# One block's attention among another block's MLP matmuls: another placement of the same work

## The chip, the cores and the metric

The kernel runs on one core of a Trainium2 chip. The metric is the device time of one execution in microseconds. Three executions of the kernel before gave 277.17, 277.19 and 277.25 us; the median is 277.19 us. Differences are read against that spread. The engines of the core work side by side, each through its own queue in order: TensorE (PE in the profile; its weight loads are PEld), VectorE (DVE), ScalarE (ACT), GpSimd (POOL) and SyncE (SP), whose queue only issues DMAs here. They meet through semaphores.

## The reference

Two layers in a row. First attention in blocks: for every batch element and head, an 8 x 8 matrix is normalized over rows and columns five times, and mixes the eight 96-row blocks of k and of v. Each block of q then attends to its own mixed block.

```python
for _ in range(5):
    P = np.exp(P - np.max(P, axis=-1, keepdims=True))
    P = P / (np.sum(P, axis=-1, keepdims=True) + 1e-09)
    P = P / (np.sum(P, axis=-2, keepdims=True) + 1e-09)
k_sorted = np.einsum('bhij,bhjcd->bhicd', P, k_b)
v_sorted = np.einsum('bhij,bhjcd->bhicd', P, v_b)
attn = softmax(scale * q_b @ k_sorted_b^T)          # within a block of 96
x = attn @ v_sorted_b                               # 4 x 768 x 512 after heads are joined
```

Then a residual MLP: a token mixing and a channel MLP.

```python
a1 = alpha1 * x + beta1
u = x + lam * np.einsum('ts,bsd->btd', w_tok, a1)
a2 = alpha2 * u + beta2
out = u + lam * (np.maximum(a2 @ w_ch1, 0.0) @ w_ch2)
```

There are 4 batch elements, 8 heads, 768 rows, head size 64, model width 512 and hidden width 2048.

## The kernel before

Every function of the kernel issues instructions through small wrappers on the engines that keep TensorE, VectorE, ScalarE and GpSimd in the order in which the program writes them (all those instructions carry line 65 in the profile, so they are told apart by tile names). DMAs that SyncE issues are not held to that order; a scheduler places them in SP's queue.

Batch element 0 has its attention done first, on its own (to about 40 us). From then on the program is a loop over batch elements b, which this text calls blocks, and over two halves `hf` of the 768 rows. A half has 16 **h units** (`h_unit`: four matmuls of 128x384 into one PSUM tile `h_ps`, then a relu on ScalarE into `hTa` or `hTb`) and 3 **ch units** (`ch_unit`: 16 matmuls of 128x512 into `ch_ps`, then the output: a multiply on VectorE into `ost`, an add on GpSimd, two DMAs out on SP).

All other work is hung between these units by a table. `put(b, hf, kind, n, ...)` (line 791) files a piece of work under a block, a half, a kind of unit ("h" or "c") and a number; `run` issues what is filed right after that unit. In the kernel before, a ch unit is cut into four parts of four matmuls, so that "c" has the numbers 0 to 11. The order within one place is the order of the `put` calls.

During block p the work of the attention of b = p + 1 is:

- `mix_matrix(b)`: a small product `repv_ps`, and six VectorE instructions that make the mixing matrices `bigM` and `bigP`. In the kernel before b = 1 is at h 10 of block 0, b = 2 and b = 3 at c 5 of half 1 of blocks 0 and 1.
- `mix_v(b, n)`, n = 0 to 2: two matmuls into `mix_ps`, then a VectorE cast of 128x1024 into `mixed`. `bounce_v` writes `mixed` to DRAM (`vscr`), `back_v` reads it back into `Vs` in another layout; both are SP's.
- `mix_k(b, n)`, n = 0 to 2: eight matmuls into `kmix_ps`, then four casts into `kT`. `q_turn_late(b, g)`, g = 0 to 3: six transposes into `qt_ps`, one copy into `qT`. These are in half 0's ch units.
- `score(b, g, hf)`, eight of them: eight matmuls into `sc_ps`, one exp on ScalarE into `et`. `pv(b, g, hf)`, eight: eight matmuls of `et` with `Vs` into `x_ps`, on VectorE a reciprocal (`rcb`), a multiply into `x`, and `first_affine`: two instructions that make `a` from `x`. In the kernel before these last two are kept back in the list `late` and issued by `flush` in the next pv, behind its multiply.
- `tails(x, lo, hi, ...)`: three VectorE copies that move rows of the last two blocks; for `a`, then for `x`.
- `moe_tok(b, kt)`: six matmuls of 128x512 into `tok_ps`, then `toktmp` and two additions into `u`. `moe_cross`: three DMA transposes of `u` into `uT`, on SP. `moe_affine`: four VectorE instructions from `uT` to `a2T`, which the next half's h units read.
- `load_kv(b + 1)` and `load_q(b + 1)`: POOL's loads for the next block.

Two PSUM pools bind these together. `psA` has two buffers of two banks each, used by `mix_ps`, `kmix_ps`, `sc_ps`, `x_ps` and `repv_ps`. `psB` has four buffers of one bank, used by `h_ps`, `ch_ps`, `tok_ps`, `qt_ps` and `back_ps`. A product can begin only when what was in its buffer has been read out.

In the scores and in pv the stationary operand has 128 columns wherever the tile has that many left, `w = min(128, ...)`, although a block has 96; the surplus rows of the output are not read. Both kernels do this.

Of the kernel before, what the change touches and what calls it, by code (L numbers as in the profile page):

```python
# [16 lines left out]
def kernel(  # L17
# [442 lines left out]
    def pv(b, g, hf):  # L460
# [17 lines left out]
            ps[0:BLK, :, :, 0:D].rearrange("p a k d -> p k a d"),  # L478
            rc[0:BLK].rearrange("p a k -> p k a").unsqueeze(3).to_broadcast([BLK, 4, 2, D]), ALU.mult,
        )  # L480
        flush()
        late.append(lambda: first_affine(b, slice(0, BLK), slice(4 * hf, 4 * hf + 4), slice(g * 128, (g + 1) * 128)))

    late = []

    def flush():
        while late:
            late.pop()()

    def tails(x, lo, hi, eng):  # L490
        flush()
        for a in range(3):
            eng(x[96:128, a:a + 4:3, lo:hi], x[32 * a:32 * a + 32, 6:8, lo:hi])

# [54 lines left out]
    def back_v(b):  # L549
        nc.sync.dma_start(Vs[b % 2][0:BLK, :, 0:D], vscr[b].rearrange("x t d -> t x d"))  # L550
# [240 lines left out]
    def put(b, hf, kind, n, *todo):  # L791
        at.setdefault((b, hf, kind, n), []).extend(todo)
# [7 lines left out]
    for ks in range(NT):  # L800
        put(0, 0, "h", ks, lambda ks=ks: prep_wtok(ks, 1, psb, (dve.tensor_copy, act.copy)[ks % 2]))
    for n in range(1, B):
        put(max(n - 2, 0), n > 1, *(("h", 10), ("c", 5))[n > 1], lambda n=n: mix_matrix(n))
    put(0, 0, "h", 9, lambda: moe_cross(0, 1))
    for g in range(CT):
        put(0, 0, "h", g, lambda g=g: first_affine(0, slice(0, 128), slice(0, NT), slice(g * 128, (g + 1) * 128)))
    for m in range(3):
        put(0, 0, "h", 10 + m, lambda m=m: first_back(m, psb))
    put(0, 0, "c", 3, lambda: moe_affine(0, 1))
    for b in range(1, B):  # L810
        p = b - 1
        off = 3 if b == 1 else 0
        for n in range(3):
            put(p, 0, "h", (13 if b == 1 else 10) + n, lambda b=b, n=n: mix_v(b, n, dve.tensor_copy))
        put(p, 0, "h", 15 if b == 1 else 12, lambda b=b: bounce_v(b))
        put(p, 0, "c", 4 if b == 1 else 0, lambda b=b: back_v(b))
        for n in range(3):
            put(p, 0, "c", off + 3 * n, lambda b=b, n=n: mix_k(b, n, ((act.copy, dve.tensor_copy)[n % 2],) * 4))
        for g in range(H4):
            put(p, 0, "c", off + (1, 4, 7, 7)[g], lambda b=b, g=g: q_turn_late(b, g, (dve.tensor_copy, act.copy, dve.tensor_copy, act.copy)[g]))  # L820
        if b + 1 < B:
            put(p, 0, "c", 11, lambda b=b: load_kv(b + 1), lambda b=b: load_q(b + 1))
        seq = [("s", 0), ("s", 1), ("s", 2), ("p", 0), ("s", 3), ("p", 1), ("p", 2), ("s", 4), ("p", 3), ("s", 5),
               ("p", 4), ("s", 6), ("p", 5), ("s", 7), ("p", 6), ("p", 7)]
        if b == 1:
            when = [("h", 0), ("h", 1), ("h", 2), ("h", 3), ("h", 4), ("h", 5), ("h", 6), ("h", 7), ("h", 8), ("h", 9),
                    ("h", 10), ("h", 11), ("h", 12), ("h", 13), ("h", 14), ("h", 15)]
        else:
            when = [("c", 8), ("c", 9), ("c", 10), ("c", 10), ("c", 11), ("c", 11), ("h", 0), ("h", 1), ("h", 2), ("h", 3),
                    ("h", 4), ("h", 5), ("h", 6), ("h", 8), ("h", 9), ("h", 11)]  # L830
        for (kind, n), (ph, at_) in zip(seq, when):
            f = (lambda b=b, n=n: score(b, n // 2, n % 2, psa)) if kind == "s" else (lambda b=b, n=n: pv(b, n // 2, n % 2))
            put(p, 1 if ph == "h" else 0, ph, at_, f)
        last = [("h", 12), ("h", 15)][b == 1]
        put(
            p, 1, *last, lambda b=b: tails(a1_of[b], 0, C, dve.tensor_copy),
            lambda b=b: tails(x_of[b], 0, C, dve.tensor_copy),
        )
# [60 lines left out]
```

## Time and profile before

| What | Value |
| --- | --- |
| median of 3 executions | 277.19 us |
| the profiled execution: its own time, its span | 277.25 us, 275.4 us |
| instructions | 5418 |
| granted TensorE clock | 1.00 |
| windows: to block 0's MLP | 0 to 39.6 us |
| block 0, half 0: h units, ch units | 39.6 to 59.7, to 72.8 us |
| block 0, half 1: h units, ch units | 72.8 to 88.4, to 105.0 us |
| block 1 begins; block 2 begins; block 3 begins | 105, 165, 225 us |

A row of the page's groups reads: line, engine, operation, output tile and input tiles, shape, count, then the busy time in us and the mean of one in ns, then the idle time of that engine just before these instructions and what ended most of it. Matmuls overlap in the machine, so that the length of one in the profile (a matmul of 128x512 is shown with 379 ns) is longer than its step (16 of them go by in 3.45 us); steps between starts are the better measure. The chain is the work that ended last, followed backwards from the end. A timeline row may stand for several instructions in a row, with the engine's idle time before them and what ended it in brackets.

### The profile page before, as it was taken

To read this page: it belongs to the slowest core of one execution; us is meant where nothing else is said; L and a number is where in the kernel's file an instruction comes from. 1 tells how busy PE (TensorE), PEld (TensorE's weight loads), DVE (VectorE), ACT (ScalarE), POOL (GpSimd) and SP (SyncE) were. 2 spreads that over 40 slices of the span, in tenths; PEclk is the share of its full clock that TensorE was granted. 3 is DMA by queue.
4 is the path that set the end of the run, shared out by engine and by line. 5 is a ranking of instruction groups with operands and counts; after the bars stand their busy time and mean duration, and the time that the engine had idled before them with its cause. 6 is when DMAs were issued, how large, how long until landed. Compare 5 with 4: busy or idle time off the path is not lost.

```text
span 275.4 us, 5418 instructions
## 1 busy us (share of the span) xinstructions
PE 262.3 (95%) x2205; PEld 141.3 (51%) x2205; DVE 166.9 (61%) x345; ACT 125.8 (46%) x231; POOL 96.6 (35%) x104
## 2 busy tenths in 40 slices
PE   8998899999999997999999999999999999999992
PEld 3466555445556443556455445555465445545540
DVE  5787527987468985476398795555689755121042
ACT  2588557225787002555777003566774004604600
POOL 8647103601471185402282456203100746022000
PEclk9999999999999999999999999999999999999999
DMA  6999999998999433339479932159300223012012
GB/s 104 215 203 196 206 207 211 171 106 185 120 186 171 29 88 94 51 89 126 91 144 183 97 75 79 38 118 126 96 10 2 76 58 79 19 38 79 0 38 76
DMA packets 60684, 29.46 MB, mean 107 GB/s; under 512 B 50082, under 2 KB 56242, under 8 KB 60660
## 3 DMA queue, kind: packets, MB, share of 16 engines
q0 software_dynamic: 26352, 15.34, 40.0%
q1 hardware_dynamic: 34308, 13.79, 26.0%
q8 instruction: 17, 0.28, 0.4%
q14 instruction: 7, 0.06, 0.1%
HBM read 32.79 MB, written 8.65 MB: 150 GB/s over the span
## 4 chain that ended last, share of the span: by engine, by line
PE 83%; DVE 9%; ACT 4%; issue 2%; DMA 1%; DVEq 0%
PE h_ps L65 29%; PE ch_ps L65 25%; PE tok_ps L65 10%; PE warm_ps L65 4%; PE x_ps L65 3%; PE sc_ps L65 3%; ACT kT L65 2%; DVE x L65 2%; DVE a L65 2%; PE kmix_ps L65 1%; PE mix_ps L65 1%; DVE ost L65 1%; PE qt_ps L65 1%; PE turn_ps L65 1%; PE v_ps L65 1%
## 5 line engine op out<-in xcount | busy, mean ns | idle before, releaser
L65 PE MATMUL h_ps<-a2T,W1p 128*128 128x384 bf16 x512 | 95.9, 326 | 1.9 <-DVE a2T L65 1.5
L65 ACT ACTIVATE hTa<-h_ps 128x384 bf16<-128x384 f32 x96 | 47.0, 492 | 90.7 <-PE h_ps L65 90.5
L65 PE MATMUL ch_ps<-W2p,hTa 128*128 128x512 bf16 x288 | 68.4, 379 | 0.0
L65 POOL TENSOR_TENSOR ost<-ost,u 128x512 f32<-128x512 f32 x21 | 26.6, 1267 | 113.9 <-DVE ost L65 108.8
L65 PEld LDWEIGHTS <-W1p 128*128 128x128 bf16 x512 | 47.3, 98 | 33.5 <-issue 2.5
L65 PEld LDWEIGHTS <-hTa 128*128 128x128 bf16 x288 | 27.2, 98 | 29.0
L65 DVE TENSOR_TENSOR ost<-ch_ps,lamB 128x512 f32<-128x512 f32 x24 | 16.6, 691 | 39.7 <-PE ch_ps L65 36.7
L65 POOL TENSOR_TENSOR u<-toktmp,x 128x512 f32<-128x512 f32 x18 | 29.3, 1640 | 8.9 <-DVE toktmp L65 8.9
L65 PE MATMUL tok_ps<-a,w_tokT 128*128 128x512 f16 x126 | 29.7, 379 | 0.0
L65 ACT ACTIVATE et<-sc_ps 96x768 f16<-96x768 f32 (+1 forms) x32 | 25.6, 811 | 2.6 <-PE sc_ps L65 2.6
L65 PE MATMUL ch_ps<-W2p,hTb 128*128 128x512 bf16 x96 | 24.6, 379 | 0.0
L65 DVE TENSOR_TENSOR toktmp<-tok_ps,lamB 128x512 f32<-128x512 f32 x21 | 14.4, 688 | 13.3 <-PE tok_ps L65 12.0
L65 ACT CAST kT<-kmix_ps 64x512 f16<-64x512 f32 x24 | 17.1, 713 | 10.0 <-PE kmix_ps L65 9.7
L65 ACT ACTIVATE hTb<-h_ps 128x384 bf16<-128x384 f32 x32 | 15.7, 490 | 9.7 <-PE h_ps L65 9.5
L65 PEld LDWEIGHTS <-w_tokT 128*128 128x128 f16 x126 | 12.2, 98 | 13.8 <-DVE a L65 0.4
L65 DVE TENSOR_TENSOR u<-toktmp,x 128x512 f16<-128x512 f32 (+1 forms) x24 | 17.7, 750 | 0.7
L65 POOL DMA_DIRECT2D qn<-in_q_dram x18 | 16.0, 924 | 5.6 <-DMA raw<-in_v_dram 5.6
L65 DVE TENSOR_TENSOR x<-x_ps,rcb 96x512 f16<-96x512 f32 x24 | 16.5, 686 | 0.8
L65 PE MATMUL x_ps<-Vs,et 96*128 96x65 f16 (+4 forms) x288 | 14.4, 195 | 2.2 <-DVE x L65 1.0
L65 PEld LDWEIGHTS <-et 96*128 96x128 f16 (+4 forms) x288 | 12.4, 100 | 7.1 <-DVE x L65 2.2
L65 DVE TENSOR_SCALAR a2T<-uT,ab2col 128x384 bf16<-128x384 f16 x28 | 11.7, 479 | 4.5 <-DMA uT<-u 4.5
L65 DVE RECIPROCAL rcb<-x_ps 96x8 f32<-96x8 f32 x24 | 4.8, 200 | 15.6 <-PE x_ps L65 15.4
(113 smaller groups left out, 255.5 us busy)
## 6 DMA issues: line engine op xcount, KB each, us to landing
out_dram<-ost SPq DMA_DIRECT2D x24, 192.0 KB, 2.3
raw<-in_v_dram POOLq DMA_DIRECT2D x6, 384.0 KB, 8.5
raw<-in_k_dram POOLq DMA_DIRECT2D x6, 384.0 KB, 9.7
qn<-in_q_dram POOLq DMA_DIRECT2D x18, 128.0 KB, 10.2
vscr<-mixed SPq DMA_DIRECT2D x6, 384.0 KB, 4.0
Vs<-vscr SPq DMA_DIRECT2D x3, 768.0 KB
W1p<-in_moe_w_ch_dram POOLq DMA_DIRECT2D x4, 512.0 KB, 12.9
W2p<-in_moe_w_ch_dram POOLq DMA_DIRECT2D x4, 512.0 KB, 17.2
```

The costliest lines, as they stand in the source:

```text
L65: ins = getattr(self.eng, name)(*args, **kwargs)
```

## The change

The operations and their shapes stay, apart from the copies of `tails`, and so does the start up to about 40 us. What changes is where the pieces are filed and which engine makes some copies:

- `ch_unit` is issued whole; "c" has the numbers 0 to 2, after 16 matmuls each.
- The three `mix_matrix` are at h 10, 11 and 12 of block 0.
- `mix_v` is at h 13 to 15 and `bounce_v` at h 15 in every block; `back_v` at c 2, though the scheduler puts it into SP's queue behind the output of the first ch unit.
- `mix_k(n)` and `q_turn_late(n)` follow ch unit n, the last two q turns both after unit 2. Of the four casts of a `mix_k` three are on ScalarE and one on VectorE (before, all four on one of them, ScalarE for n = 0 and 2); all four q copies are on ScalarE (before, two).
- All scores and pv are at h 1 to 15 of half 1. The order is s0, s1, s2, then pv0 and s3 after one unit, pv1, s4, pv2 and s5, pv3, s6, pv4 and s7, pv5, pv6, pv7.
- `late` and `flush` go; the affine of a pv follows its multiply directly. The tails of `a` are split: the first 384 columns at h 13, the others at h 15.
- The token products of half 1 come after the first whole ch unit and `moe_affine` after the second; `moe_affine(b, 1)` is at h 11 instead of 13, and in block 0 at c 0 instead of c 3.

```diff
-        flush()
-        late.append(lambda: first_affine(b, slice(0, BLK), slice(4 * hf, 4 * hf + 4), slice(g * 128, (g + 1) * 128)))
+        first_affine(b, slice(0, BLK), slice(4 * hf, 4 * hf + 4), slice(g * 128, (g + 1) * 128))
...
-        put(max(n - 2, 0), n > 1, *(("h", 10), ("c", 5))[n > 1], lambda n=n: mix_matrix(n))
+        put(0, 0, "h", 9 + n, lambda n=n: mix_matrix(n))
...
-    put(0, 0, "c", 3, lambda: moe_affine(0, 1))
+    put(0, 0, "c", 0, lambda: moe_affine(0, 1))
...
-            put(p, 0, "h", (13 if b == 1 else 10) + n, lambda b=b, n=n: mix_v(b, n, dve.tensor_copy))
-        put(p, 0, "h", 15 if b == 1 else 12, lambda b=b: bounce_v(b))
-        put(p, 0, "c", 4 if b == 1 else 0, lambda b=b: back_v(b))
+            put(p, 0, "h", 13 + n, lambda b=b, n=n: mix_v(b, n, dve.tensor_copy))
+        put(p, 0, "h", 15, lambda b=b: bounce_v(b))
+        put(p, 0, "c", 2, lambda b=b: back_v(b))
         for n in range(3):
-            put(p, 0, "c", off + 3 * n, lambda b=b, n=n: mix_k(b, n, ((act.copy, dve.tensor_copy)[n % 2],) * 4))
+            put(p, 0, "c", n, lambda b=b, n=n: mix_k(b, n, (act.copy, act.copy, act.copy, dve.tensor_copy)))
         for g in range(H4):
-            put(p, 0, "c", off + (1, 4, 7, 7)[g], lambda b=b, g=g: q_turn_late(b, g, (dve.tensor_copy, act.copy, dve.tensor_copy, act.copy)[g]))
+            put(p, 0, "c", min(g, 2), lambda b=b, g=g: q_turn_late(b, g, act.copy))
         if b + 1 < B:
-            put(p, 0, "c", 11, lambda b=b: load_kv(b + 1), lambda b=b: load_q(b + 1))
-        seq = [("s", 0), ("s", 1), ("s", 2), ("p", 0), ("s", 3), ("p", 1), ("p", 2), ("s", 4), ("p", 3), ("s", 5),
-               ("p", 4), ("s", 6), ("p", 5), ("s", 7), ("p", 6), ("p", 7)]
-        if b == 1:
-            when = [("h", 0), ("h", 1), ("h", 2), ("h", 3), ("h", 4), ("h", 5), ("h", 6), ("h", 7), ("h", 8), ("h", 9),
-                    ("h", 10), ("h", 11), ("h", 12), ("h", 13), ("h", 14), ("h", 15)]
-        else:
-            when = [("c", 8), ("c", 9), ("c", 10), ("c", 10), ("c", 11), ("c", 11), ("h", 0), ("h", 1), ("h", 2), ("h", 3),
-                    ("h", 4), ("h", 5), ("h", 6), ("h", 8), ("h", 9), ("h", 11)]
...
+            put(p, 0, "c", 2, lambda b=b: load_kv(b + 1), lambda b=b: load_q(b + 1))
+        for g in range(H4):
+            for hf in range(2):
+                put(p, 1, "h", 1 + 3 * g + hf, lambda b=b, g=g, hf=hf: score(b, g, hf, psa))
+                if g:
+                    put(p, 1, "h", 2 + 3 * g + hf, lambda b=b, g=g, hf=hf: pv(b, g - 1, hf))
+            if g == 3:
+                put(p, 1, "h", 13, lambda b=b: tails(a1_of[b], 0, 384, dve.tensor_copy))
+        put(p, 1, "h", 14, lambda b=b: pv(b, 3, 0))
+        put(p, 1, "h", 15, lambda b=b: pv(b, 3, 1), lambda b=b: tails(a1_of[b], 384, C, dve.tensor_copy), lambda b=b: tails(x_of[b], 0, C, dve.tensor_copy))
...
-            put(p, 1, "c", 5 if b == 1 else 3, lambda b=b, kt=kt: moe_tok(b, kt, psb))
-        put(p, 1, "c", 5 if b == 1 else 3, lambda b=b: moe_cross(b, 0))
-        put(p, 1, "c", 8 if b == 1 else 7, lambda b=b: moe_affine(b, 0))
+            put(p, 1, "c", 0, lambda b=b, kt=kt: moe_tok(b, kt, psb))
+        put(p, 1, "c", 0, lambda b=b: moe_cross(b, 0))
+        put(p, 1, "c", 1, lambda b=b: moe_affine(b, 0))
...
-        put(b, 0, "h", 13, lambda b=b: moe_affine(b, 1))
+        put(b, 0, "h", 11, lambda b=b: moe_affine(b, 1))
...
-                for part in range(4):
-                    ch_unit(b, hf, kk, (4 * part, 4 * part + 4))
-                    run(b, hf, "c", 4 * kk + part)
+                ch_unit(b, hf, kk)
+                run(b, hf, "c", kk)
```

More of the change, by code (lines that the diff above doesn't have):

```diff
@@ L480, in pv @@
         )
-        flush()
-        late.append(lambda: first_affine(b, slice(0, BLK), slice(4 * hf, 4 * hf + 4), slice(g * 128, (g + 1) * 128)))
[L484 to L488, printed above, removed]
+        first_affine(b, slice(0, BLK), slice(4 * hf, 4 * hf + 4), slice(g * 128, (g + 1) * 128))
     def tails(x, lo, hi, eng):
-        flush()
         for a in range(3):
@@ L808 @@
         put(0, 0, "h", 10 + m, lambda m=m: first_back(m, psb))
-    put(0, 0, "c", 3, lambda: moe_affine(0, 1))
+    put(0, 0, "c", 0, lambda: moe_affine(0, 1))
     for b in range(1, B):
         p = b - 1
-        off = 3 if b == 1 else 0
         for n in range(3):
-            put(p, 0, "h", (13 if b == 1 else 10) + n, lambda b=b, n=n: mix_v(b, n, dve.tensor_copy))
-        put(p, 0, "h", 15 if b == 1 else 12, lambda b=b: bounce_v(b))
-        put(p, 0, "c", 4 if b == 1 else 0, lambda b=b: back_v(b))
+            put(p, 0, "h", 13 + n, lambda b=b, n=n: mix_v(b, n, dve.tensor_copy))
+        put(p, 0, "h", 15, lambda b=b: bounce_v(b))
+        put(p, 0, "c", 2, lambda b=b: back_v(b))
@@ L831 @@
[L831 to L838, printed above, removed]
+            put(p, 0, "c", 2, lambda b=b: load_kv(b + 1), lambda b=b: load_q(b + 1))
```

## The prediction

> **What bounds the kernel now.** The page was read first (busy shares, chain, groups), then the windows by stage, then the chain in order of time and the timeline around the moved work. A block is one batch element b: half 0 of the MLP (16 h units, then 3 ch units), half 1 the same. Block p carries the attention of b = p + 1.
>
> ```profile
> PE 262.3 (95%) x2205; PEld 141.3 (51%) x2205; DVE 166.9 (61%) x345; ACT 125.8 (46%) x231; POOL 96.6 (35%) x104
> PE 83%; DVE 9%; ACT 4%; issue 2%; DMA 1%; DVEq 0%
> L65 ACT ACTIVATE et<-sc_ps 96x768 f16<-96x768 f32 (+1 forms) x32 | 25.6, 811 | 2.6 <-PE sc_ps L65 2.6
> L65 ACT CAST kT<-kmix_ps 64x512 f16<-64x512 f32 x24 | 17.1, 713 | 10.0 <-PE kmix_ps L65 9.7
> L65 DVE TENSOR_TENSOR x<-x_ps,rcb 96x512 f16<-96x512 f32 x24 | 16.5, 686 | 0.8
> ```
>
> TensorE is the bound. Since the change leaves every matmul in place and only reorders them, the question is how long TensorE stands still before and after. Windows by stage (us, then busy time and instructions of each engine, clock, DMA):
>
> ```profile
> core 0: us, PE busy (x) PEld busy (x) DVE busy (x) ACT busy (x) POOL busy (x), PEclk, DMA share, GB/s
> 59.70:72.76 13.06, 13.06 (x98) 7.38 (x96) 8.74 (x14) 6.09 (x10) 2.54 (x2) 1.00 1.00 148
> 88.00:105.00 17.00, 15.42 (x79) 6.92 (x77) 14.61 (x32) 0.50 (x2) 7.28 (x5) 1.00 0.56 67
> 120.90:140.20 19.30, 18.35 (x182) 10.19 (x181) 10.57 (x21) 12.95 (x19) 5.89 (x8) 1.00 0.76 122
> 140.20:150.80 10.60, 10.60 (x109) 6.45 (x108) 9.06 (x23) 7.63 (x15) 5.28 (x6) 1.00 1.22 180
> ```
>
> Little is idle: 1.6 us at 88 to 105, 0.95 at 120.9 to 140.2. The prices of TensorE's units come from the chain (start, us):
>
> ```profile
> 84.47 0.28 PE sc_ps L65 x8
> 84.74 0.76 PE h_ps L65 x4
> 85.50 0.26 PE x_ps L65 x8
> 85.76 0.65 PE h_ps L65 x4
> 148.20 2.60 PE h_ps L65 x16
> 150.81 3.45 PE ch_ps L65 x16
> 154.26 3.88 PE tok_ps L65 x18
> ```
>
> So an h unit is 0.65 (0.76 ahead of a score), a ch unit 3.45, three token products 3.88, a score 0.28, an attention product (pv) 0.26; from the same chain kmix 0.45 and a q turn 0.33. A whole block from these: 32 x 0.65 + 6 x 3.45 + 2 x 3.88 + 3 x 0.43 + 3 x 0.45 + 4 x 0.33 + 8 x 0.38 + 8 x 0.26 = 58.4. Block 1 of the profile runs from 105.1 (its h units of half 0 beginning in earnest) to 165.1, 60.0; block 2 takes 59.8. Their own stalls are thus 1.4 to 1.6 us.
>
> **Part 1: three mix_matrix at h 10 to 12 of block 0, mix_v at h 13 to 15.** Timeline of block 0's VectorE (start, us):
>
> ```profile
> 54.47 0.22 DVE L65 TENSOR_TENSOR sel<-repv_ps,mlo 128x64 f32<-128x64 f32 x1
> 55.71 1.88 DVE L65 TENSOR_TENSOR u<-back_ps,x 128x512 f32<-128x512 f32 x3
> 57.60 3.49 DVE L65 CAST mixed<-mix_ps 128x1024 f16<-128x1024 f32 x3
> ```
>
> One mix_matrix is six VectorE instructions, 54.47 to 55.71, 1.24 us. Two more come ahead of the mixed casts, which then start at 57.60 + 2.48 = 60.05 or so. mix_v's third product needs the buffer of the first cast: 60.05 + 1.22 + 0.05 = 61.3, where it stood at 59.13. The first ch unit starts at 61.8 in place of 59.7: **+2.05 us**. What these mix_matrix save later (0.13 us of TensorE, 1.2 to 2 of VectorE in c phases) lies inside stalls counted below. In blocks 1 and 2 mix_v moves from h 10 to 13 with VectorE idle before it: the transposed u lands 2.4 us after its issue (a2T at 236.10 in block 3, 11 us after h 0), before h 13. I charge nothing; bounds -0.1 to +1.2 (one cast).
>
> **Part 2: scores and pv gathered into half 1's h units.** Kept in block 0 as to place, new in blocks 1 and 2, where six of sixteen stood among the ch units. The score at h 1 now follows the last kmix by 2.0 us (two q turns 0.67, two h units 1.3); ScalarE has three kT casts and two qT copies ahead of the exps. What that looks like is in the trace (block 1, PE, then ACT):
>
> ```profile
> 131.24 0.21 PE L65 MATMUL sc_ps<-qT,kT 64*128 64x96 f16 x1
> 131.91 0.34 PE L65 MATMUL sc_ps<-qT,kT 64*128 64x96 f16 x7 [0.46 <-ACT kT L65]
> 128.95 2.91 ACT L65 CAST kT<-kmix_ps 64x512 f16<-64x512 f32 x4 [1.38 <-PE kmix_ps L65]
> 131.88 0.80 ACT L65 COPY qT<-qt_ps 128x768 f16<-128x768 f16 x1
> ```
>
> I walk it from kmix's start, with start-to-start steps of this trace: kT cast 0.72, qT copy 0.70, relu 0.38, exp 0.69, an evacuation beginning 0.25 after its matmuls (the h unit that ends at 105.77 has its relu at 106.02) and freeing its buffer 0.05 after its end (kT's last cast ends at 131.87, the score goes on at 131.91). Scores take turns on one PSUM buffer and pv on the other: each waits for the exp, or the x multiply, of the one before. Behind a waiting score stand the h units in TensorE's own queue and behind those ScalarE's relus, so time lost there is not regained.
> - ScalarE: kT 0.70 to 2.86, qT to 3.6 and 4.3, then relu, relu, exp (5.7), relu, exp (6.8), relu, relu, exp (8.3). TensorE stands 0.5 for the last kT, 0.4 at h 2 (its buffer held the third q turn), and 1.0 at the fourth score (7.4 to 8.4), which waits for the third exp. Later scores and pv wait 0.1 to 0.2 each, four times, 0.6 together. Sum 2.4 to 2.5.
> - VectorE: a pv costs 1.63 (reciprocal 0.24, multiply 0.61, the two affine steps 0.44 and 0.35), no longer with the affine pushed behind the next multiply. The first begins at 7.6; eight make 13.0, with 1.1 of gaps; the tails of a, in two goes of 3 copies (0.33 and 0.2 each, estimates scaled from 0.42 for 32x1024), add 1.6. So the a tails end near 23.4 where the first ch unit ends at 22.4. The token products wait **1.1**.
> - Bounds for both waits together: from below 0.35, what the h stage of block 0 loses now with scores and pv one to a unit; from above 6, if the 4.3 of ScalarE's backlog less the 2.0 of cover is lost whole (2.3), the scores wait as I have it (2.0) and each tail copy takes 0.42 (1.7 in all). I take 3.5, since nearly all its terms have a row.
> - After that, nothing: products, transposes and affine end near 33, the next h unit starts at 34.3. Before, block 0 paid for this chain:
>
> ```profile
> 91.90 1.32 DVE L65 COPY a<-a 32x1024 f16<-32x1024 f16 x3
> 93.25 1.29 DVE L65 COPY x<-x 32x1024 f16<-32x1024 f16 x3
> 104.63 1.30 PE L65 MATMUL h_ps<-a2T,W1p 128*128 128x384 bf16 x4 [1.54 <-DVE a2T L65]
> ```
>
> There the tokens stood after 1.5 ch units, now after one, so two ch units (6.9 us) cover tails-to-a2T. The h stage of block 0 goes from 15.84 (72.60 to 88.44) to 17.9 (16 x 0.65 + 8 x 0.38 + 8 x 0.26 = 15.5, and 2.4), +2.0; its ch stage from 16.7 (88.44 to 105.1) to 15.3, **-1.35**. Blocks 1 and 2 get 2.4 + 1.1 = 3.5 of stall for 1.4 to 1.6: **+1.9 each**.
>
> **Part 3: whole ch units, engines of the copies.** The 16 matmuls run uncut, same work. Nine kT casts on ScalarE and three on VectorE (before 8 and 4), four qT copies on ScalarE (before 2): + 0.71 + 2 x 0.70 = 2.1 us of ScalarE a block. That is hidden after ch units 0 and 1 (ScalarE is idle by the next kmix, 4.2 us on) and is in the walk after unit 2.
>
> **Part 4: queues.** back_v stands one output pair later on SP in blocks 1 and 2; in block 0 its DMA waits for the bounce, 2.45 later. There it was issued at 66.70 and the DMA share fell to nothing at 74.5, some 7.5 us; now 69.2, landing 76.7, and pv's first use is at 73.7 + 7.1 = 80.8. It is covered by 4 us, by 6 in the others; without that cover each microsecond counts one for one. POOL's loads keep their place (end of half 0), and land 45 us ahead of use.
>
> **Sum.** Block 0: +2.05 + 2.0 - 1.35 = +2.7. Blocks 1 and 2: +1.9 each. Block 3 has only moved a2T, idle on VectorE, 0. Total **+6.5**. The profiled execution took 277.25 with a span of 275.4 (1.85 around it), 0.06 over the median 277.19. So **283.7 us**.
>
> The clock is granted at 1.00 in all windows above, also in the one with two stalls of half a microsecond, so I add nothing for it. The Trainium skill ("TensorE: Matmul & The Clock Gate", section "A second HAM failure mode: psum-queue depth-cycling") speaks against such an order: frequent small idles between matmul groups that cycle through PSUM can make the clock swing to half rate. With the 3.4 us window that page gives, one window at half rate per h stage would, as an estimate, add 3 x 1.7 = 5 us and make 289.
>
> **Rivals.**
> - *ScalarE's backlog is absorbed, faster.* If the exps run ahead of my walk, the waits at scores vanish and blocks 1 and 2 keep only small stalls: -1.35 - 2 x 1.5 + 2.05 = -2.3, 274.9. It decides from the point where qT and kT clear ScalarE within 2.0 us of the last kmix; against it stands the 0.46 wait above, behind four casts that took 2.91. Chance 0.07.
> - *Only block 0's mixing is late.* Later stalls equal those replaced: +2 to +3, 280. For it: before too, scores meet busy kT casts. 0.14.
> - *VectorE becomes the bound of the h stage.* An affine multiply took 0.87 for 0.41 at 137.51 beside POOL's add. Eight of those a block add 3.7; 1 to 3 reach TensorE through pv's buffer and the token wait, three times: 287 to 291. Against it: POOL only issues loads in that stage. 0.10.
> - *back_v lands late.* A landing 4 us later than in the trace begins to cost; at 6 us, 2 us in block 0 alone: 286. 0.04.
>
> My own case has 0.62, from 281.5 to 286; no difference within 0.2% (about what this kernel's measurement can tell) 0.03. Slower by more: 0.62 + 0.14 + 0.10 + 0.04 = 0.90. The range leaves out the faster case and the far end of VectorE: 279 to 288.
>
> **What will show it.** Right: the first ch unit near 61.8; in each half 1 waits of scores for et, the largest near 1 us at the fourth; a token wait for the a tails near 1 us; no wait for a2T near 105; ch stages of half 0 unchanged at 13 us. Wrong: TensorE solid in the h stages, waits for Vs, a lower clock, or affine steps at 0.8.

## The result

The changed kernel takes 285.36 us (median of 4 executions, 285.05 to 285.59), the kernel before, run on the same chip, 277.20. The ratio is 1.0293, its 95% interval 1.0276 to 1.0311: slower by 8.2 us. The forecast was 283.7 us, between 279 and 288, and slower with a chance of 0.90.

The page of the changed kernel has these lines for those shown of the kernel before (busy shares, the chain by engine, three groups):

```profile
PE 263.6 (93%) x2205; PEld 143.1 (50%) x2205; DVE 162.7 (57%) x345; ACT 131.7 (46%) x240; POOL 96.4 (34%) x104
PE 69%; DVE 18%; ACT 9%; issue 3%; DVEq 0%
L65 ACT CAST kT<-kmix_ps 64x512 f16<-64x512 f32 x27 | 19.2, 713 | 21.0 <-PE kmix_ps L65 20.7
L65 ACT ACTIVATE et<-sc_ps 96x768 f16<-96x768 f32 (+1 forms) x32 | 26.0, 823 | 0.7
L65 DVE TENSOR_TENSOR x<-x_ps,rcb 96x512 f16<-96x512 f32 x24 | 16.5, 686 | 0.8
```

TensorE has the same 2205 matmuls, but its part of the chain falls from 83% to 69%. VectorE's goes from 9% to 18% and ScalarE's from 4% to 9%: TensorE now waits for them. The list of its waits says for what (tile waited on, tile waited for, total us, times, longest):

```profile
PE tok_ps L65 <- DVE a L65: 3.9, 3, 1.3
PE sc_ps L65 <- ACT et L65: 2.1, 3, 0.7
PE mix_ps L65 <- DVE mixed L65: 1.6, 1, 1.6
PE sc_ps L65 <- DVE kT L65: 1.6, 3, 0.5
...
PE sc_ps L65 <- ACT kT L65: 0.8, 3, 0.3
```

What comes three times comes once in each of blocks 0 to 2. The 1.5 us for a2T, which led this list before, is gone. The windows by stage (half 0's ch units of block 0, half 1's h units, half 1's ch units, and half 1's h units of block 1):

```profile
core 0: us, PE busy (x) PEld busy (x) DVE busy (x) ACT busy (x) POOL busy (x), PEclk, DMA share, GB/s
61.97:75.00 13.03, 13.03 (x97) 7.37 (x96) 7.41 (x11) 6.37 (x9) 2.61 (x3) 1.00 0.94 138
75.00:92.80 17.80, 16.25 (x196) 9.81 (x193) 10.90 (x26) 15.38 (x29) 8.58 (x11) 1.00 1.31 167
92.80:108.60 15.80, 14.52 (x73) 6.49 (x70) 13.49 (x29) 0.46 (x1) 7.19 (x5) 1.00 0.20 47
137.20:155.00 17.80, 16.25 (x196) 9.80 (x193) 10.90 (x26) 15.38 (x29) 8.56 (x11) 1.00 1.30 164
```

Each h stage of half 1 stands still for about 1.5 us, each ch stage behind it for about 1.3, and the clock stays at 1.00 through it. The timeline of TensorE in block 0 shows the places (start, us, then in brackets the idle time just before):

```profile
61.54 0.59 PE L65 MATMUL mix_ps<-raw,bigM 128*128 128x512 f16 x2 [1.60 <-DVE mixed L65]
...
75.01 1.46 PE L65 MATMUL h_ps<-a2T,W1p 128*128 128x384 bf16 x8
76.75 0.21 PE L65 MATMUL sc_ps<-qT,kT 64*128 64x96 f16 x1 [0.28 <-ACT kT L65]
77.49 0.34 PE L65 MATMUL sc_ps<-qT,kT 64*128 64x96 f16 x7 [0.53 <-DVE kT L65]
...
82.28 0.35 PE L65 MATMUL sc_ps<-qT,kT 64*128 64x96 f16 x8 [0.72 <-ACT et L65]
...
97.73 4.12 PE L65 MATMUL tok_ps<-a,w_tokT 128*128 128x512 f16 x18 [1.28 <-DVE a L65]
```

A sum by block needs one mark in each kernel. The mark taken here is the first token product of half 0 of a block: at 105.77, 165.77 and 225.54 before, at 109.24, 171.62 and 233.80 after. Counted from the first matmul of block 0's MLP (39.59 before, 39.86 after; the change begins later), block 0 is 3.20 longer, block 1 2.38, block 2 2.41, block 3 nothing. With the 0.27 of the start that is 8.26, and the spans differ by 8.3.

### The profile page after: what moved, and what is told of

The parts are those of the page before. It is cut to its first block, busy times and chain, and to the rows that moved or that the text cites. A ratio compares the mean times of both kernels' runs of the same rounds, so it can differ in the third digit from the quotient of the medians.

```text
span 283.7 us, 5430 instructions
## 1 busy us (share of the span) xinstructions
PE 263.6 (93%) x2205; PEld 143.1 (50%) x2205; DVE 162.7 (57%) x345; ACT 131.7 (46%) x240; POOL 96.4 (34%) x104
## 4 chain that ended last, share of the span: by engine, by line
PE 69%; DVE 18%; ACT 9%; issue 3%; DVEq 0%
PE ch_ps L65 26%; PE h_ps L65 19%; PE tok_ps L65 10%; DVE a L65 7%; DVE x L65 4%; PE warm_ps L65 4%; ACT kT L65 2%; ACT et L65 2%; ACT hTa L65 2%; DVE u L65 2%; PE x_ps L65 2%; ACT qT L65 2%; PE kmix_ps L65 1%; PE v_ps L65 1%; PE sc_ps L65 1%
## 5 line engine op out<-in xcount | busy, mean ns | idle before, releaser
L65 PE MATMUL ch_ps<-W2p,hTa 128*128 128x512 bf16 x288 | 66.1, 379 | 0.0
L65 PEld LDWEIGHTS <-hTa 128*128 128x128 bf16 x288 | 27.8, 98 | 31.6
L65 ACT CAST kT<-kmix_ps 64x512 f16<-64x512 f32 x27 | 19.2, 713 | 21.0 <-PE kmix_ps L65 20.7
L65 DVE TENSOR_TENSOR u<-toktmp,x 128x512 f16<-128x512 f32 (+1 forms) x24 | 19.5, 823 | 0.7
L65 DVE TENSOR_SCALAR a2T<-uT,ab2col 128x384 bf16<-128x384 f16 x28 | 9.7, 411 | 12.6 <-DMA uT<-u 12.6
L65 PE MATMUL sc_ps<-qT,kT 64*128 64x96 f16 (+1 forms) x256 | 11.5, 205 | 4.6 <-ACT et L65 2.1
```

The costliest lines, as they stand in the source:

```text
L65: ins = getattr(self.eng, name)(*args, **kwargs)
```

## The experiments

All of them are read with this ruler. "+" and "-" are us against the kernel before, in one profiled execution each; the median is over all executions, 4 to 12 of each kernel. The kernel before, run beside each group of them, had medians of 276.93 to 277.41, so differences of a few tenths between two medians of this table say nothing by themselves.

| Kernel | median us | ratio, 95% interval | block 0 | block 1 | block 2 |
| --- | --- | --- | --- | --- | --- |
| the changed kernel | 285.36 | 1.0276 to 1.0311 | +3.20 | +2.38 | +2.41 |
| a_mix | 283.30 | 1.0172 to 1.0256 | +1.32 | +2.99 | +2.45 |
| a_late | 286.00 | 1.0253 to 1.0352 | +3.41 | +2.42 | +2.64 |
| a_half | 283.65 | 1.0186 to 1.0268 | +2.82 | +1.86 | +2.05 |
| a_fine | 280.58 | 1.0068 to 1.0154 | +1.61 | +0.88 | +0.85 |
| a_fine_tok | 279.89 | 1.0082 to 1.0146 | +1.52 | +0.60 | +0.74 |
| a_all | 278.36 | 1.0032 to 1.0069 | -0.60 | +0.81 | +0.73 |
| a_all_late | 276.25 | 0.9941 to 0.9991 | -1.16 | +0.18 | +0.16 |
| b_mix | 277.39 | 0.9993 to 1.0023 | +0.57 | -0.25 | +0.01 |
| b_gather | 280.98 | 1.0120 to 1.0170 | +1.18 | +2.67 | +0.93 |
| b_mm9 | 275.40 | 0.9927 to 0.9965 | -1.55 | 0.00 | +0.01 |
| b_mm9_bank | 291.19 | 1.0470 to 1.0518 | +2.92 | +4.61 | +4.70 |
| b_mm9_k5 | 274.02 | 0.9870 to 0.9909 | -1.57 | -0.66 | -0.67 |

Names with a_ start from the changed kernel and undo something, names with b_ start from the kernel before.

### a_mix: the mixing matrices of b = 2 and 3 taken out of block 0's h units

```diff
-        put(0, 0, "h", 9 + n, lambda n=n: mix_matrix(n))
+        put(max(n - 2, 0), n > 1, *(("h", 10), ("c", 2))[n > 1], lambda n=n: mix_matrix(n))
```

> The changed kernel with the second and third mix_matrix back in ch units (after the third ch unit of half 1, blocks 0 and 1). Theory: they delay the mixed casts by 2.5 us and TensorE by 1.8 us at the third mix_v product; without them that wait goes and the first ch unit of block 0 starts near 60.0 instead of 62.0, so 283.4 us (2.0 less). Rival: VectorE's lag is only passed on, the time lost there is lost later anyway at the kT casts, and the gain is under 0.5 us (285).

Measured: 283.30, which is 2.1 less, as the theory had it. The first ch unit of block 0 starts at 59.54 instead of 61.97, and the wait for `mixed` is gone. Part 1 of the prediction holds, cause and size. Block 1 is 0.6 longer in the profiled execution, which was the longest of the four (283.92; the others 283.17 to 283.44). The product for the matrices adds some 0.2 at this place in block 0. What is new in block 1 is that SP issues an output DMA in 1.36 us instead of 0.78, the transposes of u behind it start that much later, and so does a2T. Whether this belongs to the edit or to this one execution is not shown.

### a_late: the affine deferred again

```diff
+        flush()
+        late.append(lambda: first_affine(b, slice(0, BLK), slice(4 * hf, 4 * hf + 4), slice(g * 128, (g + 1) * 128)))
-        first_affine(b, slice(0, BLK), slice(4 * hf, 4 * hf + 4), slice(g * 128, (g + 1) * 128))
...
     def tails(x, lo, hi, eng):
+        flush()
```

> The changed kernel with the affine of a pv held back behind the next pv's multiply again. Theory: an affine step that reads x right after the multiply starts 0.72 us after it instead of 0.61, so a pv costs VectorE 1.75 us instead of 1.63; eight make 0.9 us, all of it ahead of the a tails for which the token products wait. The wait falls from about 1.4 to 0.5 us in each of three blocks: 282.7 us. Rival: the wait comes from the tails cut in two and from pv starting late, and the order of the affine is worth under 0.3 us in all: 285.1.

Measured: 286.00, and a longer token wait (1.59 for 1.28). Both expectations fall, though the rival is right in that the order of the affine gains nothing. VectorE's timeline in block 0 of this kernel shows why:

```profile
82.32 0.69 DVE L65 TENSOR_TENSOR x<-x_ps,rcb 96x512 f16<-96x512 f32 x1
84.16 0.20 DVE L65 RECIPROCAL rcb<-x_ps 96x8 f32<-96x8 f32 x1 [1.15 <-PE x_ps L65]
84.39 0.69 DVE L65 TENSOR_TENSOR x<-x_ps,rcb 96x512 f16<-96x512 f32 x1
85.00 0.41 DVE L65 TENSOR_TENSOR a<-x,alphaB 96x512 f16<-96x512 f16 x1
```

The step does shrink: an affine behind another product's multiply begins 0.61 after that multiply began (84.39 to 85.00), where directly behind its own it begins 0.73 after (81.83 to 82.56 in the changed kernel). But the second product comes late here, because the fourth score, which stands ahead of it in TensorE's queue, waits for an exp, and VectorE stands still for 1.15. In the changed kernel the direct affine runs in that hole (idle there 0.24). Deferred, it is pushed out of the hole to the end, where it is missed. From the first reciprocal to the end of the tails of a VectorE takes 16.78 (82.08 to 98.86), against 16.58 in the changed kernel (81.60 to 98.18): the eight shorter steps are all eaten by the longer holes. a_all_late below tries the deferral again where VectorE had no hole.

### a_half: two of the four kT casts on each engine

```diff
-mix_k(b, n, (act.copy, act.copy, act.copy, dve.tensor_copy))
+mix_k(b, n, (act.copy, act.copy, dve.tensor_copy, dve.tensor_copy))
```

> The changed kernel with two of the four kT casts on VectorE instead of one. Theory: the casts of one PSUM tile run one after the other whichever engine has them, so kT is complete as late as before (3.5 us after kmix began, first score waiting 0.8 us), and only ScalarE's backlog is 0.7 us shorter: the wait of the fourth score (0.7) goes, 283.5 us. Rival: ScalarE's load alone sets kT; it would be complete 1.4 us earlier, the waits of the first score and the fourth go both, 281.3 us.

Measured: 283.65, as the theory had it. The timelines of ScalarE and VectorE, at block 0's last product of keys:

```profile
74.02 1.45 ACT L65 CAST kT<-kmix_ps 64x512 f16<-64x512 f32 x2 [1.97 <-PE kmix_ps L65]
...
75.51 1.45 DVE L65 CAST kT<-kmix_ps 64x512 f16<-64x512 f32 x2 [1.18 <-ACT kT L65]
```

The casts run one after the other though two engines share them: VectorE's first waits for ScalarE's second. The product began at 73.37, and the first score goes at 77.11, 3.74 later (3.60 counted to the end of that wait in the changed kernel), so nothing was gained there. What was gained is ScalarE's: it comes to the exps 0.7 earlier, and the 0.7 at the fourth score is gone.

### a_fine: ch units cut in four again, so that the last keys and q turns come earlier

```diff
-            put(p, 0, "c", n, lambda b=b, n=n: mix_k(...
+            put(p, 0, "c", 3 + 3 * n - (n == 2), lambda b=b, n=n: mix_k(...
-            put(p, 0, "c", min(g, 2), lambda b=b, g=g: q_turn_late(b, g, act.copy))
+            put(p, 0, "c", (3, 6, 9, 9)[g], lambda b=b, g=g: q_turn_late(b, g, act.copy))
...
-                ch_unit(b, hf, kk)
-                run(b, hf, "c", kk)
+                for part in range(4):
+                    ch_unit(b, hf, kk, (4 * part, 4 * part + 4))
+                    run(b, hf, "c", 4 * kk + part)
```

The other "c" numbers are translated so that they stay at the same place among the matmuls; `back_v` stands at c 4. Scores and pv stay among the h units, the casts stay 3 and 1. By the edit the last product of keys stands after one quarter of the third ch unit and the last two q turns after two; the expectation has both a quarter later.

> The changed kernel with ch units cut in four parts and kmix and the q turns spread over them (the last kmix after 2 parts of the third unit, the last two q turns one part later), scores and pv still all in the h units of half 1. Theory: ScalarE's backlog at the start of the h stage is gone, the waits of the first, second and fourth score vanish and the h stage takes 16.2 us instead of 18.5; VectorE's pv chain is not shorter, so the token wait grows from 1.4 to 1.9: 279.7 us. Rival: scores and pv gathered in one stage are themselves too much for two PSUM buffers, the h stage stays above 18 and the time above 284.

Measured: 280.58, 4.8 less than the changed kernel, 1.5 to 1.6 in each of the three blocks. TensorE in block 0:

```profile
75.31 1.46 PE L65 MATMUL h_ps<-a2T,W1p 128*128 128x384 bf16 x8
76.71 0.34 PE L65 MATMUL sc_ps<-qT,kT 64*128 64x96 f16 x8
76.98 0.82 PE L65 MATMUL h_ps<-a2T,W1p 128*128 128x384 bf16 x4
77.74 0.34 PE L65 MATMUL sc_ps<-qT,kT 64*128 64x96 f16 x8
```

No score waits any more, and the h stage takes 16.2 (75.31 to 91.53) instead of 17.8. So more than half of the loss (4.8 of 8.2) is what the lumped ch units do: the last keys and two q turns arrive together, right ahead of the first score. The token wait (1.29) is untouched, and was expected to grow.

### b_gather: only the gathering, in the kernel before

```diff
-        seq = [("s", 0), ("s", 1), ("s", 2), ("p", 0), ("s", 3), ...
-        ...
+        for g in range(H4):
+            for hf in range(2):
+                put(p, 1, "h", 1 + 3 * g + hf, lambda b=b, g=g, hf=hf: score(b, g, hf, psa))
+                if g:
+                    put(p, 1, "h", 2 + 3 * g + hf, lambda b=b, g=g, hf=hf: pv(b, g - 1, hf))
+            if g == 3:
+                put(p, 1, "h", 13, lambda b=b: tails(a1_of[b], 0, 384, dve.tensor_copy))
```

and the last two pv and the tails as in the changed kernel.

> The kernel before, with only the gathering taken over: all scores and attention products of blocks 1 and 2 stand among half 1's h units, with the tails of a in two goes, as in the changed kernel; the ch units stay cut in four, the kT casts and q copies stay as before, and the affine stays deferred. Theory: what the changed kernel loses in the h stage is the casts and copies that arrive late after whole ch units, not the gathering. So blocks 1 and 2 exchange their own stalls of 1.4 to 1.6 us for a token wait of about 1.3: 277.2, between 276.5 and 278. No wait of a score for kT above 0.4. Rival: the gathering by itself costs the +1.9 a block that the prediction put on it, in blocks 1 and 2, and block 0's h stage grows by 2: 281 to 283.

Measured: 280.98. The theory falls. The total is at the lower end of the rival's, but not made up as the rival has it. No score waits for kT, as the theory had it, but TensorE's waits now read

```profile
PE tok_ps L65 <- DVE a L65: 3.2, 2, 1.6
PE h_ps L65 <- DVE a2T L65: 2.4, 1, 2.4
```

In blocks 1 and 2 gathering puts the last products at the end of the h stage (in block 0 they stood there already, and only their order and the tails in two goes are new), so VectorE's chain (affine, tails of a, then of x, token additions, a2T) ends later. The tokens of blocks 1 and 2 follow after one ch unit and wait 1.59; in block 0 they follow after one and a half, do not wait, and the a2T behind them is late, 2.43 in place of 1.54. Block 2, +0.93, is the cleanest price of it. Block 1 adds 0.7 ahead of and in block 2's first h unit (2.19 from the last four ch matmuls to the mark, 167.70 to 169.89, where ahead of block 3 it is 1.52); VectorE does a mix_matrix ahead of a2T there. And it adds what the windows of block 1's begin show (same columns as above; the clock is the third number from the end):

```profile
106.00:108.00 2.00, 2.00 (x6) 0.83 (x6) 1.40 (x4) 0.48 (x1) 0.46 (x1) 0.50 0.45 131
...
110.00:112.00 2.00, 2.00 (x13) 1.03 (x11) 1.22 (x2) 0.98 (x2) 1.39 (x1) 1.00 0.27 86
```

Right behind the wait of 2.43 the clock is granted at 0.50 until about 109.3 (by windows of half a microsecond); six token matmuls take 2.35 instead of 1.30. This profiled execution (282.24) was the longest of four; the others took 280.46 to 281.24.

### b_mix and b_mm9: the mixing matrices in the kernel before

b_mix moves them as the change did, b_mm9 by one ch unit, behind `moe_affine`:

```diff
-        put(max(n - 2, 0), n > 1, *(("h", 10), ("c", 5))[n > 1], lambda n=n: mix_matrix(n))
+        put(0, 0, "h", 9 + n, lambda n=n: mix_matrix(n))                                      # b_mix
+        put(max(n - 2, 0), n > 1, *(("h", 10), ("c", 9))[n > 1], lambda n=n: mix_matrix(n))   # b_mm9
```

> The kernel before, with only the three mix_matrix at h 10 to 12 of block 0. Theory: the first ch unit of block 0 comes 2.05 us later, at 61.6, as in the changed kernel, but 2.5 us of VectorE work leave the chain from the tails to a2T in half 1, so that the stall of 1.54 ahead of block 1 and one of some tenths ahead of block 2 go: 277.3, between 276.8 and 278. Rival: the late start of the ch stage is lost whole and nothing comes back: 279.2.

> The kernel before, with mix_matrix of b = 2 and 3 moved from the second ch unit of half 1 to the third, behind moe_affine. Theory: the two go from VectorE's chain tails, token product, u, transposes, a2T, so the stall of 1.54 ahead of block 1 goes, and what there is ahead of block 2: 275.3, between 274.8 and 276. Rival: the chain is held by something else (the transposing DMAs, the token products) and less than 0.5 is gained: above 276.7.

Measured: 277.39 and 275.40, both as the theory had them. In b_mix the mixing waits 1.60 for `mixed`, 2.1 are lost ahead of the ch stage, and 1.23 of the 1.54 for a2T come back (0.31 is left). In b_mm9 the h unit that waited 1.54 has no wait:

```profile
102.94 1.19 PE L65 MATMUL h_ps<-a2T,W1p 128*128 128x384 bf16 x4
```

So taking mix_matrix out of a stretch where VectorE is late was worth 1.5 us (a_fine_tok to a_all) to 2.1 us (a_mix), and at the place that b_mm9 gives it no cost can be seen (block 1: 0.00).

### b_mm9_bank: kT casts split by PSUM bank

```diff
-                engs[2 * par + h2](
-                    dst[h2 * 64:h2 * 64 + 64, :, :, 8 * n:8 * n + 8, par],
+                for k in range(2):
+                    (act.copy, dve.tensor_copy)[k](
+                        dst[h2 * 64:h2 * 64 + 64, :, :, 8 * n + 4 * k:8 * n + 4 * k + 4, par],
```

and on the input side the same half, 4k to 4k + 4, of `kmix_ps`, which is one bank.

> The same, and each kT cast of 64x512 split in two of 64x256, one PSUM bank each, ScalarE on the first bank and VectorE on the second. Theory: the two engines work side by side since they touch different banks, kT is complete about 2.0 us after its product began instead of 2.9, and the stall of about 0.95 us ahead of the scores in blocks 1 and 2 goes: 273.7, between 273.2 and 274.8. Rival: a cast of half the size costs nearly as much as a whole one (0.45 or more of 0.72), or VectorE has no room among the ch units: the same as the kernel without the split, or slower, 275 to 278.

Measured: 291.19; the theory falls, and the rival was too mild. ScalarE and VectorE, from their timelines:

```profile
67.74 0.48 ACT L65 CAST kT<-kmix_ps 64x256 f16<-64x256 f32 x1 [0.54 <-DVE kT L65]
...
68.25 0.48 DVE L65 CAST kT<-kmix_ps 64x256 f16<-64x256 f32 x1 [0.54 <-ACT kT L65]
```

A half cast takes 0.48 (a whole one 0.71), and each of the eight waits for the one before on the other engine, 0.51 from start to start: 4.1 us for a kT where one engine takes 2.9. The different banks change nothing in that order. In block 1 scores then wait 1.89 and 0.81, and the clock is down to 0.51 between 138 and 140. The Trainium skill ("PSUM — Partial Sum Buffer", section "PSUM bank collisions raise a hardware error ⚠️") says that the compiler makes instructions of two engines wait for each other when they touch the same bank and the same group of 32 partitions of it. That does not explain this order: the banks differ here, and in a_half the input partitions of the two engines differ, 0 to 63 and 64 to 127. Two things are left that the waiting casts share, the tile kT that they write and the tile `kmix_ps` that they read. The trace of b_mm9_k5, the last run below, tells against kT. There the casts of two products into one kT run side by side for 0.57:

```profile
123.91 2.91 DVE L65 CAST kT<-kmix_ps 64x512 f16<-64x512 f32 x4
...
126.25 2.89 ACT L65 CAST kT<-kmix_ps 64x512 f16<-64x512 f32 x4 [0.51 <-PE kmix_ps L65]
```

The two casts that overlap (VectorE's fourth, ScalarE's first) write different partitions of kT; but so do ScalarE's second and VectorE's first in a_half, and there VectorE waited. What only the waiting ones share is one `kmix_ps`. No run gives one product two tiles, so this is an inference and not a test.

### a_fine_tok, a_all and a_all_late: the rest of the change undone in steps

a_fine_tok is a_fine with the token products after one and a half ch units; a_all also has mix_matrix behind moe_affine as in b_mm9; a_all_late also has the deferred affine of a_late and the tails of a in one go.

```diff
-            put(p, 1, "c", 3, lambda b=b, kt=kt: moe_tok(b, kt, psb))
+            put(p, 1, "c", 5, lambda b=b, kt=kt: moe_tok(b, kt, psb))                         # a_fine_tok
-        put(0, 0, "h", 9 + n, lambda n=n: mix_matrix(n))
+        put(max(n - 2, 0), n > 1, *(("h", 10), ("c", 9))[n > 1], lambda n=n: mix_matrix(n))   # a_all
-            if g == 3:
-                put(p, 1, "h", 13, lambda b=b: tails(a1_of[b], 0, 384, dve.tensor_copy))
...
-    lambda b=b: tails(a1_of[b], 384, C, dve.tensor_copy)
+    lambda b=b: tails(a1_of[b], 0, C, dve.tensor_copy)                                        # a_all_late
```

> The changed kernel with ch units cut in four (280.58 measured), and the token products of half 1 two quarters later, behind one and a half ch units, as the kernel before had it in block 0. mix_matrix stays at h 10 to 12 of block 0. Theory: the token wait of 1.29 in each of blocks 0 to 2 goes, and since mix_matrix is out of VectorE's way the chain from the tails to a2T still fits: 276.7, between 276.2 and 277.6; what is then left over the kernel before is the late mixing alone, less the stall before block 1. Rival: the wait comes back whole ahead of the next block, for a2T: 280 or more.

> The same, and mix_matrix of b = 2 and 3 at the third ch unit of half 1 of blocks 0 and 1, behind moe_affine, so that block 0's mixing is not late. Theory: 2.05 us less than the kernel without this, 274.7, between 274 and 275.6: all that the change lost came from these three, and the gathering of scores and attention products itself costs nothing against the kernel before with mix_matrix moved (275.4). Rival: gathering has a price of its own of 0.9 us in each of three blocks, which stays: 277.5 or more.

Measured: 279.89 and 278.36. The token waits go, but TensorE then waits for a2T ahead of each next block, 2.7 us in all in a_fine_tok (0.87 to 0.97 each) and 2.5 in a_all (0.67 to 0.94). The rivals' reading of both runs was the nearer one, though the wait does not come back whole (1.29 before). Most of the lateness had only moved on. VectorE at the end of block 0's products in a_all:

```profile
91.84 0.69 DVE L65 TENSOR_TENSOR x<-x_ps,rcb 96x512 f16<-96x512 f32 x1
92.57 0.42 DVE L65 TENSOR_TENSOR a<-x,alphaB 96x512 f16<-96x512 f16 x1
93.02 0.42 DVE L65 TENSOR_TENSOR a<-a,betaB 96x512 f16<-96x512 f16 x1
93.47 0.72 DVE L65 COPY a<-a 32x256 f16<-32x256 f16 x3
94.23 1.29 DVE L65 COPY x<-x 32x1024 f16<-32x1024 f16 x3
```

There is no idle time in VectorE between 79.9 and 96 of this kernel, so here each 0.12 between multiply and affine ought to count, and the tails of a take 1.09 + 0.72 in two goes where one go takes 1.32. Gathering itself may be free; that is what a_all_late asks.

> The kernel with units cut in four, tokens behind one and a half ch units and mix_matrix behind moe_affine (278.36 measured), and now the affine deferred behind the next multiply as in the kernel before, and the tails of a in one go of three copies at h 15. Scores and attention products stay gathered. Theory: what gathering seemed to cost is VectorE's extra work at the end of it, 0.49 us for tails in two goes (1.09 + 0.72 against 1.32) and 0.12 for each product whose affine follows directly; VectorE is busy without a gap there, so about 1.0 comes back in each of blocks 0 to 2, and the waits for a2T of 0.7 to 0.9 go: 275.9, between 275.3 and 276.4. Rival: the end of VectorE's chain is set by the products' place, and as with the deferral tried alone nothing comes back but the 0.49 of the tails: 276.9. Second rival: nothing comes back, 278.

Measured: 276.25 (0.9941 to 0.9991), inside the theory's range. The trace does not bear the theory out. The same stretch of VectorE's timeline, its begin and its end:

```profile
79.28 0.20 DVE L65 RECIPROCAL rcb<-x_ps 96x8 f32<-96x8 f32 x1 [0.53 <-PE x_ps L65]
...
91.12 0.41 DVE L65 TENSOR_TENSOR a<-x,alphaB 96x512 f16<-96x512 f16 x1
91.57 0.42 DVE L65 TENSOR_TENSOR a<-a,betaB 96x512 f16<-96x512 f16 x1
92.02 1.32 DVE L65 COPY a<-a 32x1024 f16<-32x1024 f16 x3
93.37 1.29 DVE L65 COPY x<-x 32x1024 f16<-32x1024 f16 x3
```

From the first reciprocal to the end of the tails of x VectorE takes 16.83 (77.83 to 94.66), where a_all takes 17.40 (78.12 to 95.52). Of these 0.57 the tails in one go are 0.49, as the first rival has it. The deferred affine saves 0.12 for each product, but VectorE now waits 0.53 and 0.23 for the second and third product, so that next to nothing is left of it. The a2T waits shrink to 1.4 in all, and the h stage of half 1 from 16.22 to 16.01; together that is the 0.56 to 0.63 that each of blocks 0 to 2 gains. Another 0.29 between the two profiled executions lies ahead of block 0's MLP, where the kernels are the same. That the median came near the theory's 275.9 is in part luck. Tails and deferral were undone together, so what each is worth to TensorE was not separated.

With the gathering, the casts' engines and the places of mix_v, back_v and `moe_affine(b, 1)` still those of the change, the kernel is a little faster than the kernel before, and 0.85 us behind b_mm9.

### b_mm9_k5: the last product of keys a quarter of a ch unit earlier

```diff
-            put(p, 0, "c", off + 3 * n, lambda b=b, n=n: mix_k(b, n, ...
+            put(p, 0, "c", off + 3 * n - (n == 2 and b > 1), lambda b=b, n=n: mix_k(b, n, ...
```

> The kernel before with mix_matrix moved behind moe_affine (275.40 measured), and the last mix_k of blocks 1 and 2 one quarter of a ch unit earlier (c 5 in place of 6). Theory: its four casts of 0.72 in a row, 2.9 us, then end 0.9 us earlier against the first score, and the two stalls of 0.46 go, with what goes with them: 274.4, between 274.0 and 274.9. Rival: the two products of keys come too close for the casts of the one before, ScalarE or VectorE is late with them, and nothing is gained: 275.2 to 276.

Measured: 274.02, ratio 0.9870 to 0.9909, as the theory had it: 1.1% less than the kernel before, and 0.66 to 0.68 in each of blocks 1 and 2 on top of b_mm9. The first score of block 1 comes without its 0.46:

```profile
128.45 1.03 PE L65 MATMUL ch_ps<-W2p,hTa 128*128 128x512 bf16 x4
129.41 0.34 PE L65 MATMUL sc_ps<-qT,kT 64*128 64x96 f16 x8
```

In these runs the casts of one product run in a row whichever engines have them; what brought kT earlier was to start it earlier.

## Why the prediction was right, step by step

The forecast +6.5 stands against +8.2 in the medians, 1.7 too little. The mechanism held: TensorE waits in the places that were named. The sizes held less well. Its steps against the profile of the changed kernel:

- **TensorE's unit prices and the account of blocks: right.** Block 3 adds nothing, and half 0's ch stages stay at 13.0.
- **Mixing late, +2.05: right.** The ch stage starts 2.41 later, 0.27 of it from the start of the execution, so +2.14; a_mix took 2.1 away. (The working has the stage begin at 59.7 before, where the trace has 59.56; with that its own sum is 2.2.)
- **h stage of half 1, 17.9: right as a sum (17.81), not in its parts.** The walk gave the last kT 0.5, the third h unit 0.4, the fourth score 1.0 and later ones 0.6. Measured: the first score loses 0.28 + 0.53 as listed, and 1.07 counted from the end of the second h unit (75.01 + 1.41) to its own end (77.76) less its own 0.28; the third h unit does not wait; the fourth score loses 0.72 as listed. What the step had wrong is the cast on VectorE. It was taken as running beside ScalarE's three, and it runs behind them. The timelines of ScalarE and VectorE in the changed kernel:

```profile
74.54 2.15 ACT L65 CAST kT<-kmix_ps 64x512 f16<-64x512 f32 x3 [1.25 <-PE kmix_ps L65]
...
76.72 0.71 DVE L65 CAST kT<-kmix_ps 64x512 f16<-64x512 f32 x1 [1.89 <-ACT kT L65]
```

  kT is complete 3.54 after its product began (73.89 to 77.43), 0.68 later than the walk had it. That the other terms were too large by about as much is luck.
- **Token wait, 1.1: the term that was mis-sized.** From the end of the ch unit (92.82 + 3.46 = 96.28) to the first token product it is 1.45, three times 0.35 too little. The working had a pv at 1.63 of VectorE and the tails at 1.6; they take 1.75 and 1.81. VectorE at the end of block 0's products:

```profile
95.83 0.69 DVE L65 TENSOR_TENSOR x<-x_ps,rcb 96x512 f16<-96x512 f32 x1
96.55 0.42 DVE L65 TENSOR_TENSOR a<-x,alphaB 96x512 f16<-96x512 f16 x1
97.00 0.42 DVE L65 TENSOR_TENSOR a<-a,betaB 96x512 f16<-96x512 f16 x1
97.46 0.72 DVE L65 COPY a<-a 32x256 f16<-32x256 f16 x3
```

  The step from a multiply to the affine that reads its result is 0.72 or 0.73. In the trace of before, where the affine belongs to another product, it was 0.61, and that row was carried over though the change removes the very thing that made it 0.61. The gaps are smaller than the walk's (some 0.7 for 1.1). The tails end at 98.18, 24.3 after the last product of keys began, where the walk had 23.4; the tokens start at 97.73 already, after the first of the last three copies, which the walk had not allowed for either. The 0.12 explains the error of the sum, not the wait: a_late and a_all_late restore the 0.61, and VectorE's stretch is hardly shorter for it, since it then waits for products.
- **a2T ahead of block 1, -1.35: right.** No such wait is left in the list, though it is close: ahead of block 2 the first h unit takes 0.83 instead of 0.65, with a2T made from 170.15 to 171.40 beside it. Measured by the mark, block 0's ch stage is 0.91 shorter, and the 0.35 of the token wait and 0.1 are the difference.
- **Covered, as said:** casts and copies behind ch units 0 and 1, back_v, POOL's loads. No wait for Vs in these stages.
- **The clock: right.** 1.00 in all the stages, with three waits of 0.3 to 0.7 and one of 1.3 in each of blocks 0 to 2. The estimate of +5 us from the page on the clock gate did not come true for this kernel.

The sum by these: three token waits 1.05, the start 0.27, and some 0.15 in each of blocks 0 to 2. Where the prediction's reason was too coarse is in what it blamed: it put the +1.9 of blocks 1 and 2 under gathering, though its own walk had most of the h stage's waits come from casts and q copies that arrive late. a_fine shows that 1.5 to 1.6 of a block's loss is due to keys and q arriving in one lump. What gathering costs depends on what stands behind it. Alone in the kernel before (b_gather) it costs 3.8 us. With the tokens after one and a half ch units, mix_matrix behind `moe_affine`, the affine deferred and the tails in one go (a_all_late against b_mm9), gathering and what else is left of the change cost 0.15 to 0.4 a block together.

Of the rivals, that only block 0's mixing is late falls: without that part a_mix still takes 283.30, and blocks 1 and 2 lose 2.4 each. In the kernel before, the late mixing alone costs 0.2 (b_mix, 277.39), since 1.23 of the 2.1 comes back in the wait for a2T and some tenths ahead of block 2. ScalarE's backlog was not absorbed: the fourth score waits for an exp in each of the three blocks. VectorE's affine steps did not stretch (0.42 throughout the h stage), and back_v was not late.

## What to carry to other kernels

When a change reorders work, take each step's duration from a row in the new order: a step whose input is made just before it is not the step that runs behind other work. Two engines that share the evacuation of one tile may run in a row; look in the trace for whether the second waits for the first before giving it credit for half. A step saved on an engine is worth nothing if the engine then waits for its next input; compare the whole stretch, from its first instruction to its last, and not the step. And where an engine's chain is late, moving its consumer mostly moves the wait: shorten the chain, or take out what need not be in it (here mix_matrix, 1.8 us for one number changed), and start the producers earlier.

## What the runs showed of the hardware

- The first affine step starts 0.72 to 0.73 after the multiply of 96x512 into `x` where it reads that multiply's result, and 0.61 after it where it reads an older one. The second affine step, which always reads the first, starts 0.45 after it; a step on other data starts 0.34 after an affine (90.66 to 91.00 in the kernel before).
- Casts of one `kmix_ps` into one `kT` never overlap across ScalarE and VectorE in these runs, whether they are shared out by partitions of the input (a_half) or by bank (b_mm9_bank). Where the next engine was free, its cast began 0.02 to 0.04 after the end of the last. Casts of two products into one `kT` did overlap, by 0.57 (b_mm9_k5).
- One wait of 2.43 us of TensorE was followed by some 3.4 us at a granted clock of 0.50 (105.9 to 109.3 in b_gather). Waits of up to 1.6 us were not, in any stage of the changed kernel, nor was one of 2.27 in block 0 of b_mm9_bank; waits of 0.82, 1.89 and 0.81 within 5 us in its block 1 were followed by 0.50 to 0.55 from 138.0 to 141.5. The Trainium skill ("TensorE: Matmul & The Clock Gate", section "A second HAM failure mode: psum-queue depth-cycling") has frequent small idles as what makes the clock swing. In this case the changed kernel, with the many small ones, kept its clock, and the drops seen follow single long waits or several in a row.
